# A top-k search's first count moved 2.5 planned microseconds later in the instruction order of a spectral filter with a routed feed-forward network

## The chip, the cores and the metric

The kernel runs on one core of a Trainium2 chip. The metric is the device time of one execution in microseconds (us). The kernel before takes 1425.91 us, the median of three runs (1425.71 to 1428.44).

## What is computed

The reference filters eight sequences of 2496 tokens with 256 channels in the frequency domain, and sends the result through a feed-forward network with eight experts. Each expert takes exactly N/8 = 2496 tokens, by one greedy pass over all (token, expert) scores in falling order.

```python
X = np.fft.rfft(x, axis=1)
y = np.fft.irfft(X * (filt_r + 1j * filt_i)[None], n=x.shape[1], axis=1)
logits = y @ w_gate                      # 19968 tokens x 8 experts
for idx in np.argsort(-logits.flatten()):
    tok, e = idx // 8, idx % 8
    if assigned[tok] >= 0 or counts[e] >= cap: continue
    assigned[tok] = e; counts[e] += 1
for e in range(8):
    out[assigned == e] = np.maximum(y[assigned == e] @ w1[e], 0.0) @ w2[e]
```

## The kernel before, in words

**Stages.** Up to about 320 us the kernel does the Fourier transforms on TensorE, with the sequences' results kept in DRAM. Up to about 402 us it finishes the inverse transform of the last sequences while the first search runs. From there to the end it runs the experts, one after the other, some 125 us each. All matrices are split into a high and a low part (`h`, `l`), and each product takes three matmuls.

**An expert.** The tokens of an expert are gathered from DRAM in 20 tiles of 128 rows (L830, on GpSimd's queue), in five groups of 512 (448 in the last). `turn` transposes two tiles at a time (L844) and splits them into `xo` (ScalarE) and `z` (VectorE, L848). For each group and each of 8 blocks of hidden units, `products` makes six matmuls of 512 columns into `pz` (L864). ScalarE writes the high part of the relu to `hl` (L891), VectorE the low part (L893; L896 in the last group). Then for each 128 tokens 24 matmuls of 256 columns make `py` (L930), ScalarE copies it (L940), and GpSimd scatters it to the output (L941). The weights of the next expert are loaded by an indirect DMA (L814) and split by ScalarE and VectorE (L823, L824).

**The searches.** Greedy assignment is done in phases: each phase fills the one expert that fills next. `Route.phase` first makes four passes over the scores (L644 to L651), then `A`, the one-hot choice of each token (L654). Then `threshold` finds the score at which the expert is full, in 11 rounds of 3 bits or less. Each round is a call of `counts`: VectorE compares all scores with 3, 7 or 9 thresholds (`Gm`, L559), TensorE counts per threshold and expert (11 or 13 small matmuls `rt<-A,Gm`, L567, "the count"), VectorE masks and adds (`t1`, `D1`, `X`, L575 to L577), TensorE sums over the partitions (`rt<-X,ones`, L580, "the sum"), and VectorE makes the next thresholds (L604 to L619, L595 to L600). The first round of a search has 3 thresholds, rounds two to ten have 7, the last has 9. There are seven such searches, in phases 0 to 6, so the third and later ones are those of phases 2 to 6; in the count's rows they are told apart by the width (48x96, 48x80, 48x64, 48x48, 48x32 for phases 2 to 6).

**The places.** After a phase's search, `places` turns the result into token numbers in five chunks. Each chunk has two pairs of matmuls `rt<-dt,GE` (L777, "a chunk pair"). From each pair VectorE takes `loc` (L778), then ScalarE adds signs twice (L781), then VectorE takes `ex` (L782). With `ex` the pair's PSUM tile is free.

**PSUM.** Counts, sums and chunk pairs all write to the PSUM tag "a", which has two tiles that are used in turn. So each of them waits until the last but one of them has been read.

**What sets the order.** TensorE's order is written out by hand: the expert's code yields estimated times, `Pump.feed` adds them to a clock, and when the clock reaches `due` it emits the next step of the search (`step_main`) or of the places (`step_side`). The generator yields a kind and a size; `s.lag` says how much later the next step is due. For a count (kind `G`) that is `LAGS[ph][0] + 0.17 * n`, for a sum (kind `X`) `LAGS[ph][1]`, n being the number of thresholds. The next search's passes are emitted once the first chunk of the places before is out; the remaining four chunks are emitted between the steps of the new search. The orders of VectorE, ScalarE and GpSimd are made by a scheduler from the emitted program; `issue_after(x)` keeps an instruction behind x in that order. `s.last` is the instruction that makes the first chunk's token numbers, and for the second search the low parts of the first expert's first rows (`R.last`, L848).

Of the kernel before, what the change touches and what calls it, by code (L numbers as in the profile page):

```python
# [9 lines left out]
AF, OP, AX = mybir.ActivationFunctionType, mybir.AluOpType, mybir.AxisListType  # L10
# [5 lines left out]
G = 22  # L16
S = B * G
# [4 lines left out]
LAGS = [(1.6, 1.2), (1.9, 1.2), (2.4, 1.4), (2.2, 1.3), (2.2, 1.2), (2.6, 1.2), (2.6, 1.2), (2.6, 1.2)]  # L22
# [111 lines left out]
class Fft:  # L134


    def __init__(s, tc, i, xs, zd, lg, pp):
        s.tc, s.nc, s.i, s.xs, s.zd, s.lg, s.pp = tc, tc.nc, i, xs, zd, lg, pp
        s.zw = s.y7 = s.y9 = s.R = None
        s.xos = []  # L140
        s.nload = s.nstore = 0
        s.st_x = s.ld_z = tc.nc.sync
        s.cps = tc.nc.vector.tensor_copy, tc.nc.scalar.copy
        s.y1c = {}
        s.Y1, s.yt, s.yd, s.z, s.xr, s.vs = {}, {}, {}, {}, {}, {}
# [321 lines left out]
class Route:  # L467
# [169 lines left out]
    def phase(s, ph):  # L637

        nc = s.nc
        v = lambda n, sh, dt=F32, bufs=2: s.wb.tile(sh, dt, name=n, bufs=bufs)  # L640

        if 0 < ph < 7:
            with s.tc.issue_after(s.last):
                nc.vector.tensor_reduce(s.M, s.lg, axis=AX.X, op=OP.max)  # L644
            yield 'd', 5.5
            nc.vector.tensor_tensor(s.tmp, s.lg, s.M.unsqueeze(2).to_broadcast([117, S, 8]), op=OP.is_equal)  # L646
            yield 'd', 1.5
            nc.vector.tensor_tensor(s.tmp, s.tmp, s.val[:117].unsqueeze(1).to_broadcast([117, S, 8]), op=OP.mult)  # L648
            yield 'd', 1.5
            nc.vector.tensor_reduce(s.ar, s.tmp, axis=AX.X, op=OP.max)  # L650
            nc.vector.scalar_tensor_tensor(s.ar, s.asg, 0.0, s.ar, op0=OP.is_equal, op1=OP.mult)  # L651
            yield 'd', 1.8
            n = s.n = 8 - ph
            nc.vector.tensor_tensor(s.A[:, :S*n].rearrange("p (s e) -> p s e", e=n), s.ar.unsqueeze(2).to_broadcast([117, S, n]),  # L654
                                    s.desc[:117, :n].unsqueeze(1).to_broadcast([117, S, n]), op=OP.is_equal)
            s.room()
            yield 'd', 1.5
        if ph < 7:
# [10 lines left out]
        if ph < 7:  # L669
            n = s.n  # L670
            T = s.T

            w, P, c, q, r1 = v("w", [128, 8]), v("P", [128, 16 * n]), v("c", [128, 2 * n]), v("q", [128, 8]), v("r1", [128, 10])
# [53 lines left out]
        with s.tc.issue_after(s.last):  # L727
            t, t3 = v("u", [117, S]), v("u2", [117, S])
# [368 lines left out]
class Pump:  # L1097
# [3 lines left out]
    def __init__(s, R):  # L1101
        s.R, s.ph, s.tags, s.out, s.limit, s.clock = R, 0, set(), {}, 0, 0.0
        s.main, s.due, s.held = R.phase(0), 0.0, False
        s.side = []
        s.on_w, s.kind = None, ''
        s.lag = dict(d=lambda t: t, G=lambda n: LAGS[s.ph][0] + 0.17 * n, X=lambda n: LAGS[s.ph][1], m=lambda t: 1.0 + 1.2*t, w=lambda t: t,
                     o=lambda t: t, p=lambda t: t, g=lambda t: 3.0)

    def step_main(s):
        if s.held:  # L1110
            if s.ph > s.limit:
                return False
            s.held = False
            tab, BE, widx = s.R.made
            xid, oid = (s.R.wb.tile([128, 20], I32, name=n, bufs=2) for n in ("xid", "oid"))
            s.out[s.ph] = (xid, oid, widx)
            s.side.append([s.clock, s.ph, s.R.places(s.ph, tab, BE, xid, oid)])
            s.on_w(s.ph)
            return True
        if s.main is None:  # L1120
            return False
        y = next(s.main, None)
        if y is None:
            s.ph += 1
            s.main = s.R.phase(s.ph) if s.ph < 8 else None
            if s.ph == 2:
                s.due = max(s.due, s.clock + 5)
            return s.main is not None
        k, t = y
        s.kind = k  # L1130
        s.held = k == 'w'
        s.due = s.clock + s.lag[k](t)
        return True
# [48 lines left out]
```

## Time and profile before

| | before |
|---|---|
| median of three runs | 1425.91 us |
| the profiled execution's own time | 1423.78 us |
| its span, first to last instruction | 1422.0 us |
| TensorE matmul busy | 1385.4 us (97%) |
| TensorE weight load busy | 1216.9 us (86%) |
| VectorE busy | 893.8 us (63%) |
| ScalarE busy | 672.0 us (47%) |
| GpSimd busy | 503.6 us (35%) |
| mean granted TensorE clock | 0.991 |

The profile is one execution. A row of a timeline gives the start, the duration, the engine, the line, the operation, output and inputs, and in brackets how long the engine had been idle before it and what ended that. Matmuls overlap each other: in a dense stretch the next one starts before the one before has ended. So a row's duration is longer than the time it takes from the stream.

### The profile page before, as it was taken

To read this page: it belongs to the slowest core of one execution; us is meant where nothing else is said; L and a number is where in the kernel's file an instruction comes from. 1 tells how busy PE (TensorE), PEld (TensorE's weight loads), DVE (VectorE), ACT (ScalarE), POOL (GpSimd) and SP (SyncE) were. 2 spreads that over 40 slices of the span, in tenths; PEclk is the share of its full clock that TensorE was granted. 3 is DMA by queue.
4 is the path that set the end of the run, shared out by engine and by line. 5 is a ranking of instruction groups with operands and counts; after the bars stand their busy time and mean duration, and the time that the engine had idled before them with its cause. 6 is when DMAs were issued, how large, how long until landed. Compare 5 with 4: busy or idle time off the path is not lost.

```text
span 1422.0 us, 27350 instructions
## 1 busy us (share of the span) xinstructions
PE 1385.4 (97%) x10412; PEld 1216.9 (86%) x10412; DVE 893.8 (63%) x2554; ACT 672.0 (47%) x1632; POOL 503.6 (35%) x562
## 2 busy tenths in 40 slices
PE   9999999999989999999999999999999999999997
PEld 8998898976467898988789889888898998898987
DVE  5577676775667777568667876866867634423231
ACT  6766676645544254236335534523623635423231
POOL 3344343443034135324322733343334324333312
PEclk9999999999989999999999999999999999999999
DMA  9665664539961022112112212112111311111100
GB/s 375 250 228 182 197 217 132 165 106 297 367 224 58 16 97 66 36 53 78 50 33 83 67 43 89 46 48 99 46 44 50 136 52 55 47 39 50 40 19 28
DMA packets 57846, 153.12 MB, mean 108 GB/s; under 512 B 11023, under 2 KB 31519, under 8 KB 54131
## 3 DMA queue, kind: packets, MB, share of 16 engines
q0 software_dynamic: 22720, 72.67, 15.6%
q1 hardware_dynamic: 29132, 73.39, 14.9%
q10 hardware_dynamic: 5863, 5.31, 1.1%
q8 instruction: 82, 1.34, 0.4%
q14 instruction: 49, 0.40, 0.1%
HBM read 88.32 MB, written 63.06 MB: 106 GB/s over the span
## 4 chain that ended last, share of the span: by engine, by line
PE 42%; issue 6%; DVE 4%; POOL 1%; ACT 1%; DMA 0%; POOLq 0%; ACTq 0%; another core or an unknown queue 0%; DVEq 0%
PE py L930 20%; PE pz L864 19%; PE ptr L844 2%; POOL out L941 1%; PE rt L567 1%; PE rt L777 1%; DVE hl L896 1%; DVE w1l L824 0%; DVE hl L893 0%; DVE M L644 0%; DVE tmp L646 0%; ACT junka L781 0%; DVE tmp L648 0%; ACT hl L891 0%; DVE Gm L559 0%
## 5 line engine op out<-in xcount | busy, mean ns | idle before, releaser
L930 PE MATMUL py<-w1h,hl 128*128 128x256 f32 x2496 | 481.6, 286 | 0.8 <-DVE hl L896 0.8
L930 PEld LDWEIGHTS py<-w1h,hl 128*128 128x128 f32 x2496 | 400.9, 191 | 3.6 <-DVE hl L896 1.2
L930 PE MATMUL py<-w1l,hl 128*128 128x256 f32 (+1 forms) x1280 | 358.1, 282 | 0.0
L941 POOL DMA_INDIRECT out<-y,oid x160 | 169.2, 1058 | 501.1 <-ACT y L940 452.6
L891 ACT ACTIVATE hl<-pz 128x512 fp32r<-128x512 f32 (+1 forms) x320 | 187.7, 588 | 229.4 <-PE pz L864 186.6
L864 PE MATMUL pz<-xo,w0h 128*128 128x512 f32 (+2 forms) x646 | 265.8, 411 | 2.7 <-DVE hl L893 1.2
L893 DVE SCALAR_TENSOR_TENSOR hl<-pz,hl 128x512 fp32r<-128x512 f32 x256 | 175.4, 687 | 139.3 <-ACT hl L891 136.5
L864 PE MATMUL pz<-xo,w0l 128*128 128x512 f32 (+2 forms) x646 | 251.5, 389 | 0.0
L864 PE MATMUL pz<-z,w0h 128*128 128x512 f32 (+2 forms) x646 | 251.1, 389 | 0.3
L930 PEld LDWEIGHTS py<-w1l,hl 128*128 128x128 f32 (+1 forms) x1280 | 239.8, 187 | 2.1
L830 POOL DMA_INDIRECT xg<-xs,xid x160 | 172.4, 1077 | 145.9 <-issue 54.8
L940 ACT COPY y<-py 128x256 f32<-128x256 f32 x152 | 56.6, 372 | 304.6 <-PE py L930 265.8
L864 PEld LDWEIGHTS pz<-xo,w0l 128*128 128x128 f32 x646 | 122.6, 190 | 24.1
L864 PEld LDWEIGHTS pz<-xo,w0h 128*128 128x128 f32 x646 | 123.8, 192 | 22.0 <-DVE hl L893 2.4
L864 PEld LDWEIGHTS pz<-z,w0h 128*128 128x128 f32 x646 | 123.5, 191 | 17.0 <-DVE z L848 0.9
L219 ACT COPY Y<-p 64x240 f32<-64x240 f32 (+1 forms) x302 | 115.3, 382 | 29.0 <-PE p L213 21.9
L237 POOL TENSOR_TENSOR P<-P 128x256 f32<-128x256 f32 x80 | 58.7, 734 | 162.8 <-DVE P L235 162.6
L559 DVE TENSOR_TENSOR Gm<-M,thr 117x1232 bf16<-117x1232 f32 (+2 forms) x80 | 104.4, 1315 | 0.2
L213 PE MATMUL p<-cS,xr 117*128 117x120 f32 x688 | 93.9, 276 | 2.8 <-ACT Y L219 1.5
L213 PEld LDWEIGHTS p<-cS,xr 117*128 117x128 f32 x688 | 85.4, 191 | 6.8 <-ACT Y L219 4.3
L229 PE MATMUL p<-cW,Y 128*128 128x128 f32 x640 | 88.4, 276 | 0.6 <-DVE Q L236 0.6
L229 PEld LDWEIGHTS p<-cW,Y 128*128 128x128 f32 x640 | 80.0, 191 | 5.7 <-issue 3.9
(229 smaller groups left out, 2013.2 us busy)
## 6 DMA issues: line engine op xcount, KB each, us to landing
zd<-zt SPq DMA_DIRECT2D x60, 256.0 KB
xs<-xo SPq DMA_DIRECT2D x17, 600.0 KB
xr<-x SPq DMA_DIRECT2D x6, 1536.0 KB
z<-zd SPq DMA_DIRECT2D x14, 600.0 KB
xr<-x SPq DMA_DIRECT2D x6, 1216.0 KB
xs<-Y SPq DMA_DIRECT2D x10, 600.0 KB
zd<-zt ACTq DMA_DIRECT2D x20, 256.0 KB
z<-zd POOLq DMA_DIRECT2D x7, 600.0 KB
```

The lines of the kernel that those rows point to most:

```text
L213: s.lastmm = nc.tensor.matmul(p[:, q-q0, :120], xv[:, q-24*h], s.cS1, start=True, stop=True).ins
L219: c = (nc.vector.tensor_copy if (t == 5 if b else cp) else nc.scalar.copy)(dst, src)
L229: nc.tensor.matmul(p[:, k], s.Y1[b][:, 4*g+k, dh*128:dh*128+128], s.cW[:, 4*g+k], start=True, stop=True)
L237: nc.gpsimd.tensor_tensor(P[:, :, :64], P[:, :, :64], P[:, :, 64:], op=OP.subtract)
L559: nc.vector.tensor_tensor(Gm[:, s0:s1, :m], s.M[:, s0:s1].unsqueeze(2).to_broadcast([117, s1 - s0, m]), thr[:117].unsqueeze(1).to_broadcas ...
L830: s.lastg = s.nc.gpsimd.indirect_dma_start(out=xg[:n], out_offset=None, in_=s.xs, in_offset=bass.IndirectOffsetOnAxis(ap=ids[0][:n, t:t+1] ...
L864: nc.tensor.matmul(p[:, a:b], w[:, sl], x[:, k, a:b], start=m == 0, stop=m == 5, skip_group_check=True)
L891: s.lasta = s.R.relu = nc.scalar.activation(h[:, :n], p[:, :n], AF.Relu).ins
L893: s.R.low = nc.vector.scalar_tensor_tensor(l[:, :n], p[:, :n], 0.0, h[:, :n].bitcast(F32), op0=OP.max, op1=OP.subtract).ins
L930: nc.tensor.matmul(p[:a.stop-a.start], hs[g][f][:, a], b[:, 256*f:256*f+256], start=m == 0, stop=m == 8 * len(terms) - 1, skip_group_check ...
L940: s.lasta = nc.scalar.copy(y, p).ins
L941: st = nc.gpsimd.indirect_dma_start(out=out_rows, out_offset=bass.IndirectOffsetOnAxis(ap=ids[1][:w, 4*g+t:4*g+t+1], axis=0), in_=y[:w], i ...
```

## The change

Three things change. In phases 1 to 6 the pass that makes `A` is put behind `s.last`. In phases 2 to 6 the first count (n = 3) falls due 2.5 units of the pump's clock later after its thresholds' comparison, and the sum that follows it 0.8 units later. Nothing is added to or removed from the work.

```diff
             n = s.n = 8 - ph
-            nc.vector.tensor_tensor(s.A[:, :S*n].rearrange("p (s e) -> p s e", e=n), s.ar.unsqueeze(2).to_broadcast([117, S, n]),
-                                    s.desc[:117, :n].unsqueeze(1).to_broadcast([117, S, n]), op=OP.is_equal)
+            with s.tc.issue_after(s.last):
+                nc.vector.tensor_tensor(s.A[:, :S*n].rearrange("p (s e) -> p s e", e=n), s.ar.unsqueeze(2).to_broadcast([117, S, n]),
+                                        s.desc[:117, :n].unsqueeze(1).to_broadcast([117, S, n]), op=OP.is_equal)
             s.room()
...
-        s.lag = dict(d=lambda t: t, G=lambda n: LAGS[s.ph][0] + 0.17 * n, X=lambda n: LAGS[s.ph][1], m=lambda t: 1.0 + 1.2*t, w=lambda t: t,
+        s.lag = dict(d=lambda t: t, G=lambda n: LAGS[s.ph][0] + 0.17 * n + (2.5 if s.opens(n) else 0), X=lambda n: LAGS[s.ph][1] + (0.8 if s.opens(n) else 0), m=lambda t: 1.0 + 1.2*t, w=lambda t: t,
                      o=lambda t: t, p=lambda t: t, g=lambda t: 3.0)
+
+    def opens(s, n):
+        return n == 3 and s.ph > 1
```

In the changed kernel the lines from 654 on have other numbers (A's pass is L655, the chunk pair L778, `turn`'s transposes L845 and low parts L849, the products L865, the relu's low parts L894, `py` L931); L567 and L580 keep theirs.

**First place: VectorE, the second search's `A`, at the start of the first expert.** `w0l` is a low part of the first expert's weights, `z` the low part of its rows, `hl` a relu's. Before:

```order
L651 SCALAR_TENSOR_TENSOR ar<-asg,ar 117x176
L654 TENSOR_TENSOR A<-ar,row 117x1232
L824 TENSOR_TENSOR w0l<-wr_5199,w0h 128x512 x2
L848 TENSOR_TENSOR z<-ptr,xo 128x2x256 x2
L824 TENSOR_TENSOR w0l<-wr_5199,w0h 128x512 x2
L893 SCALAR_TENSOR_TENSOR hl<-pz,hl 128x512 x3
```

Now:

```order
L651 SCALAR_TENSOR_TENSOR ar<-asg,ar 117x176
L825 TENSOR_TENSOR w0l<-wr_5199,w0h 128x512 x2
L849 TENSOR_TENSOR z<-ptr,xo 128x2x256 x2
L655 TENSOR_TENSOR A<-ar,row 117x1232
L825 TENSOR_TENSOR w0l<-wr_5199,w0h 128x512 x2
L894 SCALAR_TENSOR_TENSOR hl<-pz,hl 128x512 x3
```

The pass stands four instructions later; VectorE's order is then the same as before up to the third search.

**Second place: TensorE, the opening of the third search (phase 2, 48x96).** Before, the first count stood right behind a chunk pair:

```order
L930 MATMUL py<-w1l,hl 64x256
L777 LDWEIGHTS GE
L777 MATMUL rt<-dt,GE 128x180
L777 LDWEIGHTS GE
L777 MATMUL rt<-dt,GE 128x180
L567 LDWEIGHTS Gm
L567 MATMUL rt<-A,Gm 48x96
```

Now another chunk pair and product matmuls stand ahead of it:

```order
L865 MATMUL pz<-xo,w0l 128x512
L778 LDWEIGHTS GE
L778 MATMUL rt<-dt,GE 128x180
L778 LDWEIGHTS GE
L778 MATMUL rt<-dt,GE 128x180
L865 MATMUL pz<-xo,w0h 128x512
L865 MATMUL pz<-z,w0h 128x512
L865 MATMUL pz<-xo,w0l 128x512
L567 LDWEIGHTS Gm
L567 MATMUL rt<-A,Gm 48x96
```

The count has moved behind the next chunk pair, which before came between the count and its sum. In phases 3 and 6 the first count stood next to a pair in the same way, and no longer does.

**Third place: TensorE, the sum of the seventh search's first round (phase 6, 128x6).** Before:

```order
L864 MATMUL pz<-xo,w0h 128x512
L864 MATMUL pz<-z,w0h 128x512
L864 MATMUL pz<-xo,w0l 128x512
L580 LDWEIGHTS ones_3680
L580 MATMUL rt<-X_0_3682,ones_3680 128x6
L864 MATMUL pz<-xo,w0h 128x512
```

Now:

```order
L778 MATMUL rt<-dt,GE 128x180
L865 MATMUL pz<-xo,w0h 128x448
L865 MATMUL pz<-z,w0h 128x448
L865 MATMUL pz<-xo,w0l 128x448
L580 LDWEIGHTS ones_3680
L580 MATMUL rt<-X_0_3682,ones_3680 128x6
L865 MATMUL pz<-xo,w0h 128x448
L865 MATMUL pz<-z,w0h 128x448
L865 MATMUL pz<-xo,w0l 128x448
L865 MATMUL pz<-xo,w0h 128x448
L865 MATMUL pz<-z,w0h 128x448
L865 MATMUL pz<-xo,w0l 128x448
L778 LDWEIGHTS GE
```

A chunk pair now ends three product matmuls ahead of the sum, and the next pair starts six behind it.

## Rows read from the trace of the kernel before

**Rows 1.** The page: the span; busy time by engine; VectorE's busy tenths in 40 slices.
```profile
span 1422.0 us, 27350 instructions
...
PE 1385.4 (97%) x10412; PEld 1216.9 (86%) x10412; DVE 893.8 (63%) x2554; ACT 672.0 (47%) x1632; POOL 503.6 (35%) x562
...
DVE  5577676775667777568667876866867634423231
```

**Rows 2.** Timeline, TensorE: counts, sums and chunk pairs that it waited for, phases 2 to 6.
```profile
558.83 0.64 PE L567 MATMUL rt<-A,Gm 117*128 117x96 bf16 x11 [0.66 <-DVE Gm L559]
...
562.66 0.19 PE L580 MATMUL rt<-X,ones 128*128 128x42 f16 x1 [0.57 <-DVE X L577]
...
673.20 0.58 PE L567 MATMUL rt<-A,Gm 117*48 117x80 bf16 x11 [1.56 <-PE rt L777]
...
683.90 0.33 PE L777 MATMUL rt<-dt,GE 117*128 117x180 f16 x2 [0.69 <-DVE ex L782]
...
686.99 0.19 PE L580 MATMUL rt<-X,ones 128*128 128x35 f16 x1 [1.33 <-DVE X L577]
...
796.68 0.32 PE L777 MATMUL rt<-dt,GE 117*128 117x180 f16 x2 [0.80 <-DVE t L575]
...
909.31 0.46 PE L567 MATMUL rt<-A,Gm 117*48 117x48 bf16 x11 [0.96 <-remote]
...
917.10 0.45 PE L567 MATMUL rt<-A,Gm 117*128 117x48 bf16 x11 [0.32 <-DVE ex L782]
...
1022.47 0.45 PE L567 MATMUL rt<-A,Gm 117*48 117x32 bf16 x11 [0.39 <-DVE ex L782]
```

**Rows 3.** Timeline, TensorE: two chunk pairs; two product matmuls in a dense stretch.
```profile
639.50 0.39 PE L864 MATMUL pz<-xo,w0h 128*128 128x512 f32 x1
639.74 0.39 PE L864 MATMUL pz<-z,w0h 128*128 128x512 f32 x1
...
668.96 0.33 PE L777 MATMUL rt<-dt,GE 117*128 117x180 f16 x2
...
671.31 0.33 PE L777 MATMUL rt<-dt,GE 117*128 117x180 f16 x2
```

**Rows 4.** Timeline, VectorE, at the fourth search's first count.
```profile
669.45 1.06 DVE L654 TENSOR_TENSOR A<-ar,row 117x880 bf16<-117x880 f32 x1
...
672.92 0.16 DVE L778 TENSOR_TENSOR loc<-sidx,rt 128x2 f32<-128x2 f32 x1 [1.62 <-PE rt L777]
672.99 0.16 DVE L782 TENSOR_SCALAR ex<-rt 128x4 f32<-128x4 f32 x1
```

**Rows 5.** Timeline, TensorE: a chunk pair in phase 6, later in the search.
```profile
1030.52 0.33 PE L777 MATMUL rt<-dt,GE 117*128 117x180 f16 x2
```

**Rows 6.** Timeline, VectorE: that pair's `ex`; a `loc` of phase 5.
```profile
907.78 0.16 DVE L778 TENSOR_TENSOR loc<-sidx,rt 128x2 f32<-128x2 f32 x1 [2.12 <-PE rt L777]
...
1032.20 0.16 DVE L782 TENSOR_SCALAR ex<-rt 128x4 f32<-128x4 f32 x1 [0.16 <-ACT junka L781]
```

**Rows 7.** Timeline, VectorE, around the second search's `A`.
```profile
409.06 1.44 DVE L654 TENSOR_TENSOR A<-ar,row 117x1232 bf16<-117x1232 f32 x1
...
419.26 0.69 DVE L848 TENSOR_TENSOR z<-ptr,xo 128x512 fp32r<-128x512 f32 x1 [4.28 <-issue]
...
422.08 1.97 DVE L893 SCALAR_TENSOR_TENSOR hl<-pz,hl 128x512 fp32r<-128x512 f32 x3 [0.88 <-ACT hl L891]
...
425.44 0.69 DVE L893 SCALAR_TENSOR_TENSOR hl<-pz,hl 128x512 fp32r<-128x512 f32 x1 [0.74 <-ACT hl L891]
```

**Rows 8.** Timeline, TensorE: a wait of `py`; the second search's second sum.
```profile
444.97 0.22 PE L580 MATMUL rt<-X,ones 128*128 128x49 f16 x1 [2.41 <-DVE X L577]
...
668.14 0.50 PE L930 MATMUL py<-w1h,hl 128*128 128x256 f32 x2 [0.84 <-DVE hl L896]
```

**Rows 9.** Windows: length, busy time by engine, granted TensorE clock, DMA share, GB/s.
```profile
444.80:448.20 3.40, 3.23 (x13) 2.85 (x14) 2.13 (x8) 1.28 (x5) 0.87 (x1) 0.50 0.11 39
...
540.00:1175.00 635.00, 625.37 (x4573) 554.32 (x4572) 441.31 (x1466) 270.92 (x666) 231.64 (x215) 1.00 0.19 62
```

**Rows 10.** Timeline, GpSimd: the first gather for the third expert.
```profile
651.23 0.98 POOL L830 DMA_INDIRECT xg<-xs,xid  x1 [2.18 <-issue]
```

## The prediction

> **What bounds the kernel now.** I read the page first: TensorE is busy 97% of a span of 1422.0 us, no other engine more than 63% [rows 1]. So the time is the length of TensorE's stream plus its waits, and a change that neither adds nor removes work can only move waits. In the view of who waits for whom, the search and the places hold most of TensorE's waits in the expert stages, so I read TensorE's timeline around each opening of a search. There the reader is to see nine waits of 0.3 us or more, all within the first two rounds of phases 2 to 6 [rows 2]; the rounds after them show none of that size. The nine add up to 0.66 + 0.57 + 1.56 + 0.69 + 1.33 + 0.80 + 0.96 + 0.32 + 0.39 = 7.28 us. A wait costs a little more than its gap, since the matmul ahead of it ends alone: in a dense stretch products start every 0.24 us though each takes 0.39 us [rows 3], so 0.15 us more each, 1.35 us for nine. That makes 8.6 us, 0.6% of the time, and is all that this change can win.
>
> **Why the openings wait.** The largest, 1.56 us, shows the mechanism. Chunk pairs start at 668.96 and 671.31 [rows 3], and the first count comes right behind the second. It needs the PSUM tile of the first pair, and that is free only when VectorE has done its `ex`. On VectorE the pass `A` runs first (669.45, 1.06 us); then `loc` of the second pair waits 1.62 us for TensorE; behind it in the queue stands the `ex` of the first pair, at 672.99, and it ends at 673.15 [rows 4]. The count starts at 673.20. So three things meet: two PSUM tiles in turn, VectorE's backlog from the passes, and a queue in which a wait holds up what is behind it. A pair thus kept its tile 4.19 us here. Where VectorE is free, a pair started at 1030.52 has its `ex` done at 1032.36, after 1.84 us [rows 5, 6]. These two are my bounds for a pair's hold.
>
> **The first counts and what stood behind them.** In the changed order the first counts of phases 3 and 6 stand over 2 us of product matmuls behind the last pair, that of phase 5 too, and the tile that each needs was filled about 5 us earlier (in phase 2, 3.4 us), counted in matmuls of the changed order at 0.24 us for 512 columns. That is beyond the longer hold of 4.19 us in all but phase 2, where the count waited for nothing before. So 1.56 + 0.96 + 0.39 = 2.91 us go. The 0.80 us in phase 4 is a pair's wait for the first count to be read, because pair and sum followed the count within 2 us; in the new order no pair stands between count and sum there, so I take it as gone too. Together 3.71 us, and with four times 0.15 us, 4.3 us.
>
> **The second rounds.** Their own lags don't change. The 0.32 us in phase 5 goes, since the pair that stood directly ahead of that count now stands almost 3 us ahead. The 0.66 and 0.57 us of phase 2 and the 1.33 us of phase 3 are VectorE not yet done with thresholds, comparison and `X`; the low parts of relus stand between those in its queue, before and after, only in another sequence. Bounds: all stay, or all go. I take half, (0.66 + 0.57 + 1.33) / 2 = 1.28 us, because less of the places' work is mixed in. The 0.69 us in phase 3 is a pair that follows a pair with one count between; in the new order it follows one with the sum between, about 3 us apart, so I let it stay. Part: 1.60 us, with two overlaps 1.9 us.
>
> **New tight places.** In phase 6 a pair is now followed by nine product matmuls of 448 columns and the sum, then by the pair that needs its tile: 0.33 us and nine times 0.21 us (0.24 us by 448/512) and some 0.1 us for the sum, 2.3 us against a hold of 1.84 to 4.19 us. The wait is 0 to 1.9 us; I take 0.5 us, since at that place the row of phase 6 with 1.84 us is nearest. In phase 5 it is the same with 18 matmuls of 256 columns, 2.6 us: 0 to 1.6 us, taken as 0.2 us. The count of phase 2 stands 3.4 us behind the pair whose tile it takes: 0 to 0.8 us, taken as 0.2 us. Together 0.9 us, at most 4.3 us.
>
> **Late signals.** In phase 5 VectorE waited 2.12 us, until 907.78, for a chunk pair [rows 6], though such a pair takes 0.33 us; the 0.96 us of the count behind it comes from that, and its releaser is not named. Such a delay can meet any tight place. I keep a third of that wait, 0.3 us.
>
> **The second search's pass.** `A` of phase 1 (1.44 us at 409.06) moves behind the second `z`, which ends at 419.95 [rows 7]. It was made in time in which VectorE would have been idle; now it pushes back two weight parts and the relus' low parts. Two idle times of 0.88 and 0.74 us before those low parts [rows 7] take up 1.62 us, more than the pass. The first low parts come up to 0.6 us later, and four tiles of `pz` lie between them and TensorE. I cost it at nothing; without that cover it is 0.6 us. A gain is excluded, as what followed it waited for others.
>
> **What moves with it.** The searches hang together, so the 3.3 us add up: the passes, the first chunk and the weight loads come some 3 us later in phase 2 and some 16 us in phase 6. The first gather for the third expert is issued at 651.23 [rows 10], over 20 us ahead of its first rows' transposes, which stand behind the count of 673.20. Scatters and gathers change places on GpSimd's queue by one to three positions. VectorE's busy share falls off in the last eight slices [rows 1], after the last search, so nothing there is pushed past the end. I cost all this at nothing.
>
> **Sum.** 4.3 + 1.9 - 0.9 - 0.3 = 5.0 us. The profiled execution took 1423.78 us, so it would take 1418.8 us. It lies 2.1 us under the median of 1425.91 us; I carry the saving to the median: **1420.9 us**.
>
> **The clock.** After the second search's wait of 2.41 us [rows 8] the granted clock was 0.50 for 3.40 us [rows 9], the lower of its two levels, which costs 1.7 us. From 540 to 1175 us, with all nine waits in it, it was 1.00 [rows 9]. So the waits won back bring no clock with them. [...] That wait of 2.41 us lies in phase 1, which the change leaves in its place; I leave it.
>
> **Rival 1: the waits move.** The delay adds no PSUM tile and takes nothing from VectorE. If pairs hold their tiles as long as near the passes, the new tight places cost up to 4.3 us and the second rounds give nothing back. Then 4.3 + 0.5 (phase 5's second count) - 4.3 us leaves 0.5 us: 1425.4 us. For it speaks that the pair after the first count waited before wherever it was near (0.69 and 0.80 us); against it, that the holds late in a search are short. [...]
>
> **Rival 2: slower.** The four passes and the weights' splits meet the last group's low parts (L896) at an expert's end. Once before, `py` waited 0.84 us for such a low part [rows 8]. The shift puts the passes up to 16 us closer to the expert's end. If in all five phases the low parts come late by the four passes' usual excess, about that 0.84 us and another `A`-sized pass of 1.06 us [rows 4], that is 1.9 us each, 9.5 us in all; less the 5.0 us of gains, 4.5 us slower: **1430.4 us**. It decides when VectorE's queue at the expert's end is over 1 us behind the relus in more than two phases. Against it: only one of five phases shows such a wait now, and VectorE is at 70% of the stretch from 540 to 1175 us (441.31 of 635.00 us) [rows 9].
>
> **Chances.** The forecast, faster by several us: 0.58. Waits that move, 1425.4 us: 0.31. Slower: 0.11. About 0.2%, 2.9 us, is what a measurement of this kernel tells from no change; the forecast's lower half would still pass it. The likeliest case's own range is 1417.3 (all 8.6 us) to 1423.0 us; with rival 1 and the bounds of the unknown waits the range that should hold 8 in 10 is 1416.8 to 1427.5 us.
>
> **What would show it.** Right: the first counts of phases 3, 5 and 6 start without a gap, and TensorE's waits for L577, L559 and chunk pairs in phases 2 to 6 add up to about 2 us instead of 7.28 us. Rival 1: as much waiting as before, at chunk pairs and second sums. Rival 2: `py` rows behind L896 with gaps. Wrong at the root: the openings run clean and the time stays, which would mean that the gaps of the profiled execution are not those of the timed runs.

## The result and the profile after

The changed kernel took 1445.36 us (median of four runs, 1441.83 to 1446.73), the kernel before 1427.18 us beside it (1425.71 to 1431.5): ratio 1.0117, 95% interval 1.0096 to 1.0138. It is slower by some 18 us, where 5 us less was forecast and the range ended at 1427.5 us. The profiled execution took 1445.7 us. Its page, first lines, against [rows 1]:

```profile
span 1443.9 us, 27348 instructions
...
PE 1391.3 (96%) x10412; PEld 1218.2 (84%) x10412; DVE 893.5 (62%) x2554; ACT 670.1 (46%) x1632; POOL 499.1 (35%) x562
```

No engine does more work; TensorE has 5.9 us more of busy time, and the span is 21.9 us longer between these two executions (18.2 us between the medians). To see where, I cut both runs at the first transpose of each expert. The columns are the stretch, its length, the busy time of PE, PEld, DVE, ACT and POOL, the granted clock, DMA share and GB/s. The kernel before, second to sixth expert:

```profile
544.19:674.52 130.33, 126.70 (x921) 111.89 (x920) 89.97 (x289) 53.66 (x134) 46.53 (x43) 1.00 0.18 58
674.52:803.53 129.01, 125.61 (x925) 110.92 (x924) 91.98 (x304) 54.00 (x133) 47.77 (x42) 1.00 0.18 57
803.53:930.95 127.42, 125.35 (x937) 110.85 (x935) 94.31 (x313) 54.60 (x136) 44.84 (x42) 1.00 0.17 58
930.95:1055.19 124.24, 123.85 (x923) 109.67 (x922) 91.87 (x300) 53.41 (x130) 44.87 (x42) 1.00 0.18 59
1055.19:1176.15 120.96, 120.81 (x852) 108.10 (x850) 69.55 (x247) 53.06 (x126) 44.18 (x44) 1.00 0.23 78
```

The changed kernel, the same five experts, the rest, and three short stretches:

```profile
545.48:672.09 126.61, 125.46 (x906) 110.89 (x905) 86.18 (x272) 50.86 (x120) 42.95 (x40) 1.00 0.17 56
672.09:807.06 134.97, 128.13 (x912) 112.46 (x911) 92.11 (x298) 55.13 (x138) 45.87 (x45) 0.97 0.17 56
807.06:937.73 130.67, 126.48 (x928) 109.83 (x927) 91.39 (x308) 55.11 (x143) 44.52 (x44) 1.00 0.18 57
937.73:1068.51 130.78, 126.21 (x934) 111.49 (x933) 90.84 (x303) 54.17 (x134) 47.90 (x43) 0.99 0.17 57
1068.51:1197.87 129.36, 123.59 (x876) 109.73 (x875) 76.63 (x271) 52.30 (x126) 43.51 (x44) 0.99 0.22 73
1197.87:1443.90 246.03, 237.71 (x1567) 216.19 (x1565) 79.86 (x181) 85.18 (x191) 72.60 (x75) 0.99 0.12 40
682.80:689.70 6.90, 6.06 (x24) 4.19 (x22) 2.29 (x8) 1.56 (x3) 2.19 (x3) 0.51 0.19 57
1048.00:1051.50 3.50, 3.50 (x16) 3.38 (x14) 1.47 (x9) 1.44 (x5) 0.65 (x1) 0.51 0.10 37
1078.80:1082.20 3.40, 3.39 (x9) 2.72 (x9) 2.71 (x7) 0.42 (x1) 0.85 (x1) 0.50 0.09 22
```

The second expert is 3.7 us shorter, the next four are 6.0, 3.3, 6.5 and 8.4 us longer: 20.4 of the 21.9 us. TensorE's idle time (length less busy time) grew from 9.6 to 22.5 us in these five. The three short stretches with a granted clock of 0.51, 0.51 and 0.50 are new: from 540 to 1175 us the kernel before had one of 1.00 [rows 9]. In the third of them products start every 0.43 us (at 1079.84, 1080.27 and 1080.69), where in [rows 3] they start every 0.24 us. If the stretches cost the share of the clock that was not granted, that is 6.8 us, an estimate.

In TensorE's timeline of the changed kernel the first counts look nearly as forecast: those of phases 2, 3, 5 and 6 (117x96, 117x80, 117x48 and 117x32) start without a gap; only phase 4's is split by 0.51 us. But waits stand at other places:

```profile
555.26 0.65 PE L567 MATMUL rt<-A,Gm 117*48 117x96 bf16 x11
...
681.22 0.49 PE L865 MATMUL pz<-xo,w0h 128*128 128x512 f32 x1 [2.97 <-issue]
...
682.61 0.77 PE L567 MATMUL rt<-A,Gm 117*48 117x80 bf16 x11
...
796.77 0.44 PE L865 MATMUL pz<-xo,w0h 128*128 128x448 f32 x1 [1.27 <-DVE hl L897]
...
803.77 0.51 PE L931 MATMUL py<-w1h,hl 128*128 128x256 f32 x2 [1.16 <-DVE hl L897]
...
812.29 0.24 PE L567 MATMUL rt<-A,Gm 117*48 117x64 bf16 x2 [0.51 <-issue]
...
930.44 0.45 PE L567 MATMUL rt<-A,Gm 117*48 117x48 bf16 x11
...
1047.19 0.33 PE L778 MATMUL rt<-dt,GE 117*128 117x180 f16 x2 [2.21 <-DVE ex L783]
...
1051.66 0.45 PE L567 MATMUL rt<-A,Gm 117*48 117x32 bf16 x11
...
1078.81 0.17 PE L580 MATMUL rt<-X,ones 128*128 128x14 f16 x1 [2.64 <-DVE X L577]
```

The clock falls right behind the three largest of them, at 681.22, 1047.19 and 1078.81. Counts, sums and chunk pairs together waited 8.7 us in these experts (waits of 0.3 us or more), where the prediction had about 2 us as its sign of being right. My first theory was S: the accumulated shift brings passes, places and rounds to the expert's end, and TensorE waits there. Its rivals: O, the later counts and sums do it themselves; A, the pass's move does.

### The profile page after: what moved, and what is told of

It reads as the page before. It is cut to its first block, busy times and chain, and to the rows that moved or that the text cites. A ratio compares the mean times of both kernels' runs of the same rounds, so it can differ in the third digit from the quotient of the medians.

```text
span 1443.9 us, 27348 instructions
## 1 busy us (share of the span) xinstructions
PE 1391.3 (96%) x10412; PEld 1218.2 (84%) x10412; DVE 893.5 (62%) x2554; ACT 670.1 (46%) x1632; POOL 499.1 (35%) x562
## 4 chain that ended last, share of the span: by engine, by line
PE 81%; issue 6%; DVE 6%; ACT 3%; DMA 2%; POOL 1%; another core or an unknown queue 1%; POOLq 0%; DVEq 0%; ACTq 0%
PE py L931 26%; PE pz L865 26%; PE p L213 5%; PE p L229 5%; PE pa L284 4%; PE pv L395 3%; PE pa L248 2%; PE ptr L845 2%; PE rt L567 2%; DMA xs<-Y 2%; PE pv L257 2%; POOL out L942 1%; PE rt L778 1%; DVE hl L897 1%
## 5 line engine op out<-in xcount | busy, mean ns | idle before, releaser
L931 PE MATMUL py<-w1h,hl 128*128 128x256 f32 x2496 | 482.5, 286 | 2.7 <-issue 1.5
L931 PEld LDWEIGHTS py<-w1h,hl 128*128 128x128 f32 x2496 | 401.4, 191 | 5.1 <-issue 1.6
L931 PE MATMUL py<-w1l,hl 128*128 128x256 f32 (+1 forms) x1280 | 358.5, 282 | 0.4 <-issue 0.4
L865 PE MATMUL pz<-xo,w0h 128*128 128x512 f32 (+2 forms) x646 | 266.9, 413 | 9.6 <-issue 3.0
L865 PE MATMUL pz<-z,w0h 128*128 128x512 f32 (+2 forms) x646 | 252.8, 391 | 3.4 <-issue 1.3
L865 PE MATMUL pz<-xo,w0l 128*128 128x512 f32 (+2 forms) x646 | 253.1, 392 | 0.0
L894 DVE SCALAR_TENSOR_TENSOR hl<-pz,hl 128x512 fp32r<-128x512 f32 x256 | 175.1, 688 | 125.1 <-ACT hl L892 123.5
L931 PEld LDWEIGHTS py<-w1l,hl 128*128 128x128 f32 (+1 forms) x1280 | 240.4, 188 | 2.3 <-issue 0.5
L831 POOL DMA_INDIRECT xg<-xs,xid x160 | 167.0, 1044 | 136.0 <-PE ptr L845 47.7
L865 PEld LDWEIGHTS pz<-xo,w0h 128*128 128x128 f32 x646 | 124.2, 192 | 33.6 <-issue 6.3
L865 PEld LDWEIGHTS pz<-xo,w0l 128*128 128x128 f32 x646 | 123.5, 191 | 24.7 <-issue 0.4
L865 PEld LDWEIGHTS pz<-z,w0h 128*128 128x128 f32 x646 | 124.2, 192 | 21.7 <-DVE z L849 2.0
```

The lines of the kernel that those rows point to most:

```text
L831: s.lastg = s.nc.gpsimd.indirect_dma_start(out=xg[:n], out_offset=None, in_=s.xs, in_offset=bass.IndirectOffsetOnAxis(ap=ids[0][:n, t:t+1] ...
L865: nc.tensor.matmul(p[:, a:b], w[:, sl], x[:, k, a:b], start=m == 0, stop=m == 5, skip_group_check=True)
L894: s.R.low = nc.vector.scalar_tensor_tensor(l[:, :n], p[:, :n], 0.0, h[:, :n].bitcast(F32), op0=OP.max, op1=OP.subtract).ins
L931: nc.tensor.matmul(p[:a.stop-a.start], hs[g][f][:, a], b[:, 256*f:256*f+256], start=m == 0, stop=m == 8 * len(terms) - 1, skip_group_check ...
```

## The experiments

The jobs ran on five chips, which the results number 10, 1, 0, 11 and 14; the chip of the first comparison has no number. Each chip was used by one job alone, so what goes with a chip here could also go with its job. Where a run was made turned out to matter more than any edit.

### One part at a time (chip 10)

e1 is the hunk on the pass `A` alone, e2 the hunk on `s.lag` alone. e3 shifts each search by as much as the change, but leaves first counts and sums their lags:

```diff
-                     ... m=lambda t: 1.0 + 1.2*t, w=lambda t: t,
+                     ... m=lambda t: 1.0 + 1.2*t, w=lambda t: t + (3.3 if s.ph > 1 else 0),
```

e4 is the whole change with the delay in one phase:

```diff
     def opens(s, n):
-        return n == 3 and s.ph > 1
+        return n == 3 and s.ph == 2
```

> Only the move of the pass A behind s.last, in phases 1 to 6; no later count or sum. Theory S (the loss is the accumulated shift of the searches' passes and places against the experts): 1427 us, within 0.2% of before, since nothing is shifted. Theory O (the loss is at the delayed openings themselves): the same, 1427 us. Theory A (A's place behind VectorE's other work makes the first count's operand late in each phase): above 1435 us.

> Only the later first count (2.5) and its sum (0.8) of phases 2 to 6; A stays where it was. S and O: 1445 us, as the whole change, within 3 us. A: below 1432 us.

> The first count and sum keep their lags, but the search of each phase from 2 on starts 3.3 units later, so that passes, places and weight loads shift against the experts by the same accumulated amount as in the change (3.3 in phase 2 to 16.5 in phase 6). S: slower than before by most of the change's loss, 1440 to 1448 us. O: 1427 us, within 3 us, with the waits at first counts that the kernel before has.

> The whole change, but its delays in phase 2 alone, so that every later search is shifted by the same 3.3 units and none by more. S: the loss grows with the shift, so about a fifth to a third of the change's loss in each phase: 1428 to 1433 us. O: the loss belongs to each delayed opening, so phase 2's part alone: the first expert's stretch 3.7 us shorter and the rest as before, 1424 us. If the loss is not in the accumulation but in any shift at all: 1440 us or more.

Measured, against 1411.74 us for before on that chip: e1 1411.63 us, ratio 1.0001 (0.9989 to 1.0013); e2 1412.12, 1.0006 (0.9995 to 1.0016); e3 1412.78, 1.0011 (0.9997 to 1.0026); e4 1409.08, 0.9992 (0.9979 to 1.0006). No part loses anything that can be told, S, O and A all fail there, and the kernel before is itself 15 us faster than in the first comparison. Either the parts lose only together, or the loss belongs to the chip or the job.

### The whole change, before again, and VectorE held up (chip 1)

e5 and e6 are the two kernels unchanged. e7 and e8 add a reduction in front of the second pair of the first two chunks (it came to fourteen times, 2.81 us each, not twelve):

```diff
+                if ch < 2 and t == 2 and ph > 0:
+                    with s.tc.issue_after(s.lex):
+                        nc.vector.tensor_reduce(v("blk", [117, 5]), s.iota.unsqueeze(1).to_broadcast([117, 5, 512]), axis=AX.X, op=OP.add)
                 nc.vector.tensor_tensor(loc[:, u], s.sidx[:, u], pr[:, :, S], op=OP.subtract)
```

> The changed kernel as it is, on the same chip and beside the same runs of before as the next three. Theory C (the loss comes from late results of TensorE, which the records of the first comparison show and those of the four single parts do not): where no late results show, 1408 to 1414 us when before takes 1412, ratio 0.997 to 1.003; where they show, ratio about 1.012. Theory I (the pass's move and the later counts lose together what neither loses alone): 1425 to 1431 us when before takes 1412, ratio about 1.012 on any chip, with TensorE's idle time in the second to sixth expert near 22 us.

> The kernel before, unchanged, for its own profile on this chip. Theory C: no late results of TensorE and under 6 us of TensorE idle in the second to sixth expert (9.6 us in the first comparison); ratio 1.000. Theory I: the same, 1.000.

> The kernel before, with a reduction of 5 x 512 elements (about 3 us of VectorE, its result unused) between the first and the second pair of the first two chunks of the places of phases 1 to 6: twelve times VectorE is held up where a late result would hold it up. Theory C: 5 to 15 us slower than before, as the searches' openings are near those pairs. If VectorE has room there: under 3 us.

> The changed kernel with the same twelve reductions. If the changed order is the more sensitive to VectorE held up near the openings: its loss against e5_whole is 10 us or more above that of e7 against before. If the change only met more late results: both lose the same within 3 us. If the delay gives room: it loses less than e7 does.

The whole change took 1411.55 us against 1412.28, ratio 0.9991 (0.9981 to 1.0001); e6 0.9996 (0.998 to 1.0012; one of its ten executions took 3451.94 us, for a reason that no run shows, and is left out). So theory I falls: on this chip the change is neither faster nor slower by what can be told, as theory C had it where no late results show (they are explained below). The profile of e6 shows why nothing was to be won. Its TensorE timeline, at the places of [rows 2] in the same program:

```profile
556.17 0.64 PE L567 MATMUL rt<-A,Gm 117*128 117x96 bf16 x11
559.88 0.19 PE L580 MATMUL rt<-X,ones 128*128 128x42 f16 x1 [0.45 <-DVE X L577]
...
669.34 0.57 PE L567 MATMUL rt<-A,Gm 117*48 117x80 bf16 x11 [0.32 <-DVE ex L782]
...
679.18 0.33 PE L777 MATMUL rt<-dt,GE 117*128 117x180 f16 x2
680.79 0.19 PE L580 MATMUL rt<-X,ones 128*128 128x35 f16 x1
...
789.93 0.32 PE L777 MATMUL rt<-dt,GE 117*128 117x180 f16 x2 [0.76 <-DVE t L575]
...
901.53 0.45 PE L567 MATMUL rt<-A,Gm 117*48 117x48 bf16 x11
...
909.06 0.45 PE L567 MATMUL rt<-A,Gm 117*128 117x48 bf16 x11 [0.32 <-DVE ex L782]
...
1014.43 0.45 PE L567 MATMUL rt<-A,Gm 117*48 117x32 bf16 x11 [0.39 <-DVE ex L782]
```

The nine waits, 7.28 us before, are five here, 0.45 + 0.32 + 0.76 + 0.32 + 0.39 = 2.24 us. In e5 the waits of 0.2 us or more at openings of phases 2 to 6 come to 1.22 us (0.34, 0.36, 0.22 and 0.30), and its longest wait in these experts is at an expert's end, behind a low part, in place of 0.98 us in e6. All of TensorE's waits of 0.2 us or more from 540 to 1200 us come to 3.5 us in e6 and 3.5 us in e5: what the openings win comes back elsewhere. The longest wait of e5:

```profile
791.39 0.50 PE L931 MATMUL py<-w1h,hl 128*128 128x256 f32 x2 [1.16 <-DVE hl L897]
```

What the same instructions did in the two executions of the changed kernel shows what differs. Its `py`, the chunk pair behind it, and their readers on ScalarE and VectorE, in the first comparison (three answers, by engine):

```profile
675.47 0.28 PE L931 MATMUL py<-w1h,hl 128*128 128x256 f32 x1
...
676.03 0.32 PE L778 MATMUL rt<-dt,GE 117*128 117x180 f16 x2
...
679.16 0.37 ACT L941 COPY y<-py 128x256 f32<-128x256 f32 x1 [3.60 <-PE py L931]
680.58 0.59 ACT L848 CAST xo<-ptr 128x512 fp32r<-128x512 f32 x1 [1.05 <-remote]
...
680.63 0.16 DVE L779 TENSOR_TENSOR loc<-sidx,rt 128x2 f32<-128x2 f32 x1 [4.88 <-remote]
```

And in e5:

```profile
671.76 0.28 PE L931 MATMUL py<-w1h,hl 128*128 128x256 f32 x1
...
672.32 0.32 PE L778 MATMUL rt<-dt,GE 117*128 117x180 f16 x2
...
674.39 0.39 PE L865 MATMUL pz<-xo,w0h 128*128 128x512 f32 x1
...
672.09 0.37 ACT L941 COPY y<-py 128x256 f32<-128x256 f32 x1 [0.23 <-PE py L931]
672.52 0.59 ACT L848 CAST xo<-ptr 128x512 fp32r<-128x512 f32 x1
...
672.68 0.16 DVE L779 TENSOR_TENSOR loc<-sidx,rt 128x2 f32<-128x2 f32 x1 [0.63 <-PE rt L778]
```

In e5 the copy starts 0.33 us after the last matmul of its `py` has started, in the first comparison 3.69 us after it, and both engines stand still meanwhile. `xo` is late with the copy, and the product behind them waits 2.97 us (at 674.39 in e5 it starts without a wait). I call such a thing a late result: a row on ScalarE or VectorE that reads a tile of TensorE and no other engine's result, and before which its engine stood idle over 0.5 us longer than in the undisturbed run of the same program (`ex` is left out, as it also waits for ScalarE). After 400 us the first comparison has 23 of them in the kernel before, 28 us in sum, and 36 in the changed one, 66 us. Some of that idle time is TensorE's own waiting: 17 (22 us) and 29 (56 us) of them also start over 0.5 us later after the start of the matmul that they read. Two undisturbed chips against each other (e1 against e6, which differ in the pass's place alone) leave one, of 0.7 us.

So a dense TensorE timeline doesn't tell when its readers start: the last matmul of this `py` is recorded with 0.28 us in both runs, and the copy starts 0.33 us after its start in one and 3.69 us in the other.

e7 took 1436.80 us, 24.5 us over before, where I had expected 5 to 15 us; e8 took 1430.25 us, 18.7 us over e5. Of TensorE's waits, the largest groups (in total, times, longest) for a pair in e7 and, second, in e8; ahead of them the reduction itself in e7:

```profile
L780 DVE TENSOR_REDUCE blk<-iota 117x5 f32<-117x2560 f16 x14 | 39.3, 2808 | 0.0
```

```profile
PE rt L777 <- DVE ex L785: 10.8, 6, 2.8
```

```profile
PE rt L778 <- DVE ex L786: 7.4, 5, 2.8
```

So with VectorE held up at the pairs the changed order loses 5.8 us less, and the waits at the pairs are 3.4 us less. That fits what the delay was meant to do, though e8 has the whole change and the delay wasn't tried alone. More sensitive at those pairs the changed order is not.

### On a chip with late results (chip 0)

e9 delays phases 2 and 4 (`s.ph in (2, 4)`), e10 is e4 and e11 is e5 once more.

> The whole change, its delays in phases 2 and 4 alone. On a chip without late results of TensorE, e5_whole against e6_before_again gives 2.34 us back in the second expert and 0.88 us in the fourth, and loses 0.16, 0.94 and 0.98 us in the third, fifth and sixth. If each opening's gain or loss is its own: 3 us faster than before, ratio 0.998. If the accumulated shift of 6.6 units costs: 0.9985 to 1.000. If late results of TensorE show on this chip: over 1.003.

> e4_ph2_only once more, with more rounds. If its 2.7 us were real: ratio 0.998 to 0.999 with an interval under 1. If not: 1.000.

> The changed kernel as it is, once more, on whichever chip this job gets. Theory C: ratio 0.998 to 1.001 if the records show no late results of TensorE, and 1.008 or more if they show some forty again. If the order itself were slower on one chip in several: over 1.008 without late results.

This chip gave 1427.15 us for before, as in the first comparison. e11: 1446.68 us, ratio 1.0153 (1.0125 to 1.018); e9: 1437.74, 1.0079 (1.0051 to 1.0107); e10: 1434.93, 1.005 (1.0031 to 1.007). e9 and e11 came out as expected for a chip with late results (over 1.003, and 1.008 or more); of e10 neither forecast held, and its 2.7 us and e9's 3 us can't be judged on this chip. Against the undisturbed runs of their programs e10 has 28 late results of 51 us in sum, e11 37 of 69 us: with 28, 51 and 66 to 69 us go 1427, 1435 and 1445 to 1447 us. 31 of the 36 late results of the changed kernel in the first comparison come again in e11, in the same instructions:

```profile
681.96 0.37 ACT L941 COPY y<-py 128x256 f32<-128x256 f32 x1 [5.04 <-remote]
683.36 0.58 ACT L848 CAST xo<-ptr 128x512 fp32r<-128x512 f32 x1 [1.03 <-remote]
...
683.41 0.16 DVE L779 TENSOR_TENSOR loc<-sidx,rt 128x2 f32<-128x2 f32 x1 [6.30 <-remote]
...
684.00 0.79 PE L865 MATMUL pz<-xo,w0h 128*128 128x512 f32 x1 [4.38 <-issue]
```

So they are no noise of one execution: the program decides where they come, and whether they come goes with the chip, or with its job. e10's stretches, second to sixth expert, show where it loses:

```profile
549.37:676.07 126.70, 125.51 (x907) 110.93 (x906) 86.15 (x272) 50.98 (x120) 43.00 (x40) 1.00 0.17 56
676.07:808.41 132.34, 128.29 (x927) 112.51 (x926) 93.47 (x318) 56.88 (x145) 50.29 (x46) 0.99 0.19 60
808.41:939.94 131.53, 126.77 (x938) 111.86 (x937) 94.94 (x314) 55.27 (x138) 43.88 (x42) 0.99 0.17 56
939.94:1067.23 127.29, 124.49 (x935) 110.31 (x934) 92.55 (x302) 53.54 (x130) 43.94 (x42) 1.00 0.18 58
1067.23:1188.83 121.60, 121.02 (x852) 108.11 (x851) 69.23 (x247) 52.61 (x126) 43.79 (x44) 1.00 0.24 78
```

Against the kernel before in the first comparison: 3.6 us shorter in the expert of the delayed opening, then 3.3, 4.1, 3.1 and 0.6 us longer, where phases 3 to 6 have their old lags and stand 3.3 units later (and `A` behind `s.last`). So in those experts a later opening is not needed for the loss: a shifted order with the pass's move is enough. That speaks for S on such a chip, but the pass's move isn't separated there, and the kernel before was not profiled in that job.

### The shift and short matmuls (chips 11 and 14)

e12 and e16 are e3 again, e13 is e1. e14 and e17 put extra small matmuls into the last expert's `py`, e15 and e18 behind its products:

```diff
+        def extra():
+            p = s.ps.tile([128, 180], F32, name="rt", tag="a", bufs=2)
+            for _ in range(11):
+                nc.tensor.matmul(p[:117, :32], s.R.tri[:, 118:], s.R.tri[:, 118:150], start=True, stop=True)
...
                     if f in ((3,) if half else (1, 3, 5)):
                         yield 0.65
+                    if e == 7 and f in (1, 5):
+                        extra()
```

> e3_shift_only once more: first counts and sums keep their lags, and each search from phase 2 on starts 3.3 units later. On a chip whose records show late results of TensorE (as those of the first comparison and of e9 to e11): theory S (the loss comes with the accumulated shift, which brings pairs, passes and first rounds to the expert's end) gives ratio 1.010 or more; theory O (it comes with the later counts themselves) 1.000 to 1.003. On a chip without: 1.001 as in e3, and nothing is told.

> e1_a_only once more: only the pass's move. On a chip with late results: 1.000 (S and O), over 1.004 if the move has a part in the loss. On one without: 1.000 as in e1.

> The kernel before, with 40 times 11 small matmuls (32 columns, result unused) in the last expert, where nothing is searched: two sets in each block that makes py. Each set should cost about 0.5 us, 20 us in all. Theory D (on some chips TensorE's results come late after a long stretch of short matmuls, as at an expert's end with pairs and counts mixed in): on such a chip the last expert is longer than e15's by 5 us or more, with late results in it; on the others the two cost the same within 3 us.

> The same 40 sets, one behind each block of products in the last expert, where the matmuls are twice as long. About 0.5 us each, 20 us in all, on either kind of chip; theory D: no late results at the products. If late results come with any small matmuls: as many as in e14.

> e3_shift_only a third time, for a chip with late results of TensorE. There, theory S: ratio 1.010 or more, with the losses in the third to sixth expert; e10 speaks for it, whose phases 3 to 6 are only shifted by 3.3 units and whose third to fifth expert were 3 to 4 us longer than those of before in the first comparison. Theory O: 1.000 to 1.003. On a chip without late results: 1.000 again, and nothing is told.

> e14 once more. On a chip with late results, theory D: 5 us or more slower against before than the 26 us of e14, with late results in the last expert. On one without: ratio 1.018 again.

> e15 once more. On a chip with late results, theory D: 25 us slower as in e15, within 3 us; if late results come with any small matmuls, as much more as e17. On one without: ratio 1.017 again.

Both chips were without late results (before 1411.54 and 1411.71 us). Ratios: e12 0.9999 (0.9987 to 1.0011), e16 1.0004 (0.9994 to 1.0015), e13 0.9996 (0.9985 to 1.0006); e14 1.018 and e17 1.017, e15 1.0171 and e18 1.0174, some 25 to 26 us for the 40 sets where 20 us had been expected. The shift and the pass's move are free there, a third time and a second, and small matmuls cost the same in either place. What these would do on a chip like 0 stays open: theory D has neither been borne out nor refuted.

## Why the prediction was wrong

Two steps failed: the gain was read from waits that are mostly not the program's ("What bounds the kernel now"), and the loss was left out, as "Late signals" at 0.3 us and "What moves with it" at nothing.

**What bounds the kernel now.** The nine waits were read from one execution, with late results in it, and taken as what the order costs. In the same program elsewhere they are 2.24 us, with five overlaps 3.0 us, and not 8.6 us. The 1.56, 1.33 and 0.96 us, the three largest, are 0.32 us and nothing. So the terms of 4.3 and 1.9 us were oversized by what the late results had put in; on an undisturbed chip the change gives at the openings 2.24 less 1.22, 1.0 us, and takes it back elsewhere: 0.9991.

**Late signals.** I had seen one (the 2.12 us at 907.78, [rows 6]), and kept 0.3 us for it. In the first comparison this term is the one that decides: 36 late results of 66 us in the changed kernel against 23 of 28 us, and with them 12.9 us more of TensorE's idle time in the second to sixth expert and 6.8 us of clock. One chain from a late result to a wait is shown above (2.97 us); that they set the sign as a whole is argued from the two comparisons of the same program that have them (1.0117 and 1.0153) and the one that has none (0.9991). Why the changed order meets more of them is open.

**What moves with it.** Costed at nothing, and rightly on three chips, by what can be told: 1.0011, 0.9999 and 1.0004 for the shift alone. With late results it fails: e10's experts with nothing but the shift and the pass's move are 3.3, 4.1, 3.1 and 0.6 us longer.

**The clock.** "The waits won back bring no clock with them" held (in e5 and e6 the granted clock is 1.00 in each of the second to sixth experts); that waits could be added and cost clock was not considered. Some 6.8 us, the estimate above, went so, behind waits of 2.97, 2.21 and 2.64 us.

**New tight places and second rounds.** On the undisturbed chip both were sized too high. None of the three new tight places that the prediction names has a wait of 0.2 us in e5, where 0.9 us was put on them. The 1.22 us of e5 stand at the second sums of phases 3, 4 and 6 (0.88 us) and at one chunk pair ahead of phase 3's search (0.34 us), where the prediction let 2.0 us of the second rounds stay. **The second search's pass** costs nothing that can be told on two undisturbed chips (1.0001, 0.9996, with `A` moved in all six phases).

**The rivals.** Rival 2 had the sign, but not the mechanism. Its sign, `py` behind L897, shows once (1.16 us), as 0.98 us did in e6, and two products waited 1.27 and 0.41 us for such low parts; that is no 9.5 us. Rival 1, waits that move, is what happens on the undisturbed chip, at a lower price: about 1 us changes place. Three of the four waits that [rows 2] put down to a reader of a tile kept their length in e6 (0.76, 0.32 and 0.39 us), so these are the program's own. By the prediction's own reading the 1.56 us is a wait for a tile as well, and in e6 it is 0.32 us. Most of the three largest of the nine went with the late results, and was no lack of tiles.

**The last sentence** of the prediction, that gaps of the profiled execution might not be those of other runs, came closest. The mechanism (two tiles, a queue in order) was right, as e7's 10.8 us and e8's 7.4 us of waits for `ex` show; what held up VectorE in the largest waits was late results more than its own backlog.

## What to carry to other kernels

Before a wait is costed, ask whether it is the program's: profile the unchanged kernel on a second chip and keep only the waits that come back. If a reader stands idle long after the matmul that it waits for (3.69 us here against 0.33 us), what is tuned may be the habit of one chip or job, and another order meets such places otherwise (23 in the kernel before, 36 in the changed one). Compare changes of under 2% on more than one chip: this one is 1.2 to 1.5% slower in two comparisons and, by what can be told, the same in a third (0.9991).

## What the runs showed of the hardware

The kernel before takes 1411.5 to 1412.3 us on four chips and 1427 us on chip 0, with the same work; 15 us, 1.1%. On chip 0 and in the first comparison TensorE's results come up to 5.7 us late (6.30 us of idle time before the `loc` at 683.41 in e11, 0.63 us in e5), and 31 of the changed kernel's 36 late results come again in e11, in the same instructions. Those shown above are of a `py`, and of the transposes and the chunk pair behind it. On that chip and in the first comparison the records also lack some 15% of the semaphore events (12,056 in before against 14,102 in e6, 11,872 in the changed kernel and 11,862 in e11 against 14,083 in e5, counted from the traces), while as many instructions are recorded (27,348 in each run of the changed kernel). Releasers that read "remote" or "issue" go with it: 55 of the waits of over 0.15 us of TensorE, ScalarE and VectorE in e11, 2 in e5.

Why is open, and so is whether it belongs to the chip itself. Each time here is that of an execution that was recorded, so no run tells what the recording costs.
